# DeltaNet with a mixture of depths on one core: more filler products in TensorE's planned pauses, first k loads over two DMA queues, other planning costs

## Chip, cores, metric

The kernel runs on one NeuronCore of a Trainium2 chip, in one launch. The metric is the device time of that launch in microseconds, the median of its runs. Before the change it is 312.81 us (three runs, 311.75 to 313.92).

## What is computed

Attention of the DeltaNet kind over 4 batches, 8 heads, 768 tokens and a head size of 48, all in fp32, then a feed-forward block that only the 128 best-scored tokens of each batch pass through.

```python
k_n = k / (np.linalg.norm(k, axis=-1, keepdims=True) + 1e-06)
for t in range(S):                                    # S = 768
    y[:, :, t] = einsum('bhd,bhde->bhe', q[:, :, t], state)
    v_old = einsum('bhde,bhd->bhe', state, k_n[:, :, t])
    state += beta[:, :, t] * einsum('bhd,bhe->bhde', k_n[:, :, t], v[:, :, t] - v_old)
x = y.transpose(0, 2, 1, 3).reshape(B, S, H * D)      # 4 x 768 x 384
for b in range(B):
    scores = x[b] @ w_gate
    top = the 128 tokens with the highest scores
    h = maximum(x[b, top] @ w1, 0)                    # 384 x 1024
    out[b, top] = x[b, top] + sigmoid(scores[top]) * (h @ w2)
```

## The kernel before

**Tiling.** The tokens are cut into chunks of 64, 12 per sequence. Two batches are worked on together, so there are 24 steps, each one chunk of 16 heads and batch pairs. Within a chunk the token-by-token recurrence becomes a triangular system. Four steps form one elimination, of which there are six: each inverts 32x32 triangular blocks on VectorE by 30 column steps of two instructions (`step`, L760 and L764), on the copy in PSUM that ScalarE makes (`fill`, L737). There is only one such PSUM tile, `pa`.

**A step's course.** `load` (L539, L542) brings k, q and v, two DMAs each, one for each half of the partitions. `turn` transposes k and q on TensorE (L560), ACT copies them out (L564). `products_g` (L578) and `products_p` (L588) make k k^T and k q^T; ACT copies them to `g` (L598) and `p` (L602), GpSimd masks `p` (L609). `eliminate` scales the block on GpSimd (L724; on VectorE for elimination 0), opens with L737, runs its steps, and ends with L783 and the transposes L789 and L795. `join` completes each 64x64 inverse with 32x32 products (L907, L919), which ACT copies (L913, L925). `recur` is the recurrence: v scaled by the norms on GpSimd (L951), L976 and L961 (v minus what the state holds), L993 (times the inverse), ACT's copy L998 to `wbd`, L1006 (new state), L1022 and L1033 (the output), ACT's copy L1039, the output DMA L1043. `depths` picks the tokens of a batch and runs the feed-forward block (L1276 and L1290), after an indirect gather (L1260); a scatter that adds (L1299) ends it.

**What sets the order.** All instructions are issued by a planner in the kernel itself, `Plan`, when the kernel is built. Each operation has an engine, a cost in us that is written by hand, dependences and the buffers that it takes and gives back. `rank` makes 90 trial orders with priorities that partly come from a seeded random source and keeps the one whose planned end is earliest; `order` makes it. Costs thus do not only describe: a changed cost gives another order on every engine. Each engine then takes its instructions strictly in the planned order, whatever the real times are.

**Fillers.** `Plan.fill` goes over TensorE's planned order. `near` is the activity of the last 3.4 us of plan, each operation weighted with a hand-written `rate`. Where it is under a threshold, a filler is put in: two products of `warm` with itself (L1389), 128x128 in bf16, whose result nobody reads. They have no dependences and run as soon as TensorE comes to them.

The two helpers that carry a load are these:

```python
n["l" + nm] = moved(sp, 1.3, 1.5, load(i, nm), prio=u - 30 + (nm == "q") * 34,
                    take=[(nm, i)], lat=2.5)
n["mp"] = pool(1.1, mask_p(i), [n["w", 0], n["w", 1], N["masks"]], 10 * i - 10)
r["vh"] = pool(1.05, vh, [n["lv"], N["e", e]["nn"]], u - 8)
```

`moved` plans an issue on SP (1.3 us for the two DMAs), then the transfer (1.5 us) and a latency (2.5 us). A second path of `eliminate`, with 16-row quarters, is written out but its list of eliminations, `PARTED`, is empty.

Of the kernel before, what the change touches and what calls it, by code (L numbers as in the profile page):

```python
# [16 lines left out]
P = 128  # L17
# [15 lines left out]
class Plan:  # L33
# [61 lines left out]
    def fill(self):  # L95
# [5 lines left out]
        for op in ops + [None]:  # L101
            end = op.start if op else last
            here = 0
            while t + 0.12 < end or here < 2:
                if any(a < t < b for a, b in used):
                    if t + 0.12 >= end:
                        break
                    t += 0.1
                    continue
                near = sum((min(y, t) - max(x, t - 3.4)) * r for x, y, r in work[-60:]  # L110
                           if y > t - 3.4)
                if near < 2.8 and (t > 3.4 or t + 0.12 < end):
                    fill = Op()
                    fill.eng, fill.start, fill.end, fill.give, fill.seq = "PE", t, t, [], -1
                    fills.append(fill)
                    work.append((t - 0.11, t, 3.2))
                    here += 1
                elif t + 0.12 >= end:
                    break
                if t + 0.12 < end:  # L120
                    t += 0.12
# [147 lines left out]
def kernel(  # L269
# [64 lines left out]
    QC = HC // 2  # L334
    QD = QC * HC + QC
    NW = 3
    SUMS = ()
    PARTED = ()
# [22 lines left out]
    ring("a", 2, [HC * HC + QC * 2])  # L361
# [70 lines left out]
    zq = sbuf("zq", [NB // 2, QC, 2])  # L432
    identb = sbuf("identb", [P], BF16)
    low_i = sbuf("low_i", [GP, QC], BF16)
# [41 lines left out]

    def quarters():
        nc.gpsimd.tensor_copy(identb, ident)
        for x in range(2):
            nc.gpsimd.tensor_tensor(out=low_i[:, x], in0=ident[:, x * C + QC:x * C + HC],  # L480
                                    in1=ident[:, x * C + HC + QC:(x + 1) * C], op=ALU.add)
        nc.gpsimd.tensor_tensor(out=low_i[:, 0], in0=low_i[:, 0], in1=low_i[:, 1], op=ALU.add)
        nc.gpsimd.tensor_copy(low_i[:, 1:], low_i[:, :1].to_broadcast([P, GP - 1, QC]))
# [48 lines left out]
    def load(i, nm):  # L532
        g, c = divmod(i, NCH)

        def emit():
            t = got(nm, i)
            for x in range(2):
                if nm == "v":
                    nc.sync.dma_start(out=t[half[x]], in_=v[g * GB + x, :, c * C:(c + 1) * C]  # L539
                                      .rearrange("h s d -> s h d"))  # L540
                else:
                    nc.sync.dma_start(  # L542
# [4 lines left out]
    N = {}  # L547

# [86 lines left out]
    def prep(i):  # L635
# [3 lines left out]
        for nm in "kq":  # L639
            n["l" + nm] = moved(sp, 1.3, 1.5, load(i, nm), prio=u - 30 + (nm == "q") * 34,  # L640
                                take=[(nm, i)], lat=2.5)
# [15 lines left out]
        n["mp"] = pool(1.1, mask_p(i), [n["w", 0], n["w", 1], N["masks"]], 10 * i - 10)  # L657
# [8 lines left out]
    def eliminate(e):  # L666
# [4 lines left out]
        parted = e in PARTED  # L671
# [4 lines left out]
        def quarter(t):  # L676

            return (t[:, :2 * QD].rearrange("p (s x) -> p s x", x=QD)[:, :, :QC * HC]
                    .rearrange("p s (i c) -> p s i c", c=HC)[:, :, :, :QC])

        def turn_in():
            nc.vector.transpose(
                out=rows(got("a", e)[:, :HC * HC]).rearrange("p t (n x) -> p t n x", x=2),
                in_=got(*gk(e))[:, :, HC:].rearrange("p n t x -> p t n x"))

        def square():
            eng.tensor_scalar_max(nrm[:, 0], got("a", e)[:, :HC * HC:HC + 1], 1e-30)
# [17 lines left out]
        def clear():  # L705
            if parted:
                for x in range(2):
                    a = quarter(got("a", e))[:, x]
                    nc.gpsimd.affine_select(out=a, in_=a, pattern=[[1, QC], [-1, QC]], base=0,
                                            channel_multiplier=0, compare_op=ALU.is_gt, fill=0.0)  # L710
                return
            a = rows(got("a", e)[:, :HC * HC])
# [3 lines left out]
        def scale():  # L716
            if parted:
                a = quarter(got("a", e))
                eng.tensor_tensor(
                    out=a, in0=a, op=ALU.mult, in1=bh[e % 2].rearrange("p (s i) -> p s i", s=2)  # L720
                    [:, :, :, None].to_broadcast([P, 2, QC, QC]))
            else:
                a = rows(got("a", e)[:, :HC * HC])
                eng.tensor_tensor(out=a, in0=a, op=ALU.mult,  # L724
                                  in1=bh[e % 2][:, :, None].to_broadcast([P, HC, HC]))
            eng.memset(got("a", e)[:, :HC * HC:HC + 1], -1.0)

        def state():

            return (got("A", e)[:, :QC].rearrange("p i c -> p (i c)")  # L730
                    .rearrange("p (s i c) -> p s i c", s=2, c=QC))

        def fill():
            if parted:
                nc.scalar.copy(state(), quarter(got("a", e)))
                return
            nc.scalar.copy(got("A", e), rows(got("a", e)[:, :HC * HC]))  # L737

        def step_q(j):
            w = QC - 1 - j  # L740

            def emit():
                a, x = quarter(got("a", e)), state()
                t = tmp[:, :2 * w * j].rearrange("p (s i c) -> p s i c", s=2, c=j)
                nc.vector.tensor_tensor(
                    out=t, op=ALU.mult,
                    in0=a[:, :, j + 1:, j:j + 1].to_broadcast([P, 2, w, j]),
                    in1=x[:, :, j:j + 1, :j].to_broadcast([P, 2, w, j]))
                nc.vector.tensor_tensor(out=x[:, :, j + 1:, :j], in0=x[:, :, j + 1:, :j],
                                        in1=t, op=ALU.subtract)  # L750
            return emit, 0.42 + 1.9e-3 * 2 * w * j

        def step(j):
            w = HC - 1 - j

            def emit():
                a = rows(got("a", e)[:, :HC * HC])
# [10 lines left out]
        def final():  # L768

            if parted:  # L770
                a = got("a", e)
                for x in range(2):
                    i0 = x * QC * HC
                    nc.vector.tensor_tensor(
                        out=a[:, i0:i0 + QC * HC].rearrange("p (i y) -> p i y", y=2 * HC)
                        [:, :, x * HC:(x + 1) * HC].rearrange("p i (c x) -> p i x c", x=2),
                        in0=state()[:, x].rearrange("p (i x) c -> p i x c", x=2), op=ALU.mult,
                        in1=bh[e % 2][:, None, None, x * QC:(x + 1) * QC]
                        .to_broadcast([P, QC // 2, 2, QC]))
                    nc.vector.memset(a[:, i0:i0 + QC * HC].rearrange("p (i y) -> p i y", y=2 * HC)  # L780
                                     [:, :, HC - x * HC:2 * HC - x * HC], 0.0)
                return
            nc.vector.tensor_tensor(  # L783
                out=got("a", e)[:, :HC * HC].rearrange("p (i c x) -> p i x c", c=HC, x=2),
# [3 lines left out]
        def turn_out():  # L788
            nc.vector.transpose(  # L789
                out=got("tt", e)[:, :, HC:].rearrange("p n t x -> p t n x"),  # L790
                in_=got("a", e)[:, :HC * HC].rearrange("p (i c x) -> p i x c", c=HC, x=2))

        def turn_back():
# [3 lines left out]
                in_=got("a", e)[:, :HC * HC].rearrange("p (i c x) -> p c i x", c=HC, x=2))  # L797

        def keep():

            nc.gpsimd.tensor_copy(zq, got(*gk(e))[:, :, HC:HC + QC])
# [16 lines left out]
        last = on((1.9 if e == 0 else 2.2) * (0.55 if parted else 1), scale, [s["sc"], cl],  # L818
                  -650 if e else u)
        if parted:  # L820
            s["kp"] = pool(0.8, keep, [s["in"], N.get("jq")], -640)
        last = act(0.6 if parted else 1.0, fill, [last], -600, take=[("A", e)])
        for j in range(1, (QC if parted else HC) - 1):
            emit, dur = (step_q if parted else step)(j)
            last = dve(dur, emit, [last, N.get(("e", e - 1), {}).get("tb")], u)
        s["fi"] = last = dve(1.4 if parted else 1.25, final, [last], u, give=[("A", e)])
        s["to"] = last = dve(1.3, turn_out, [last], u, take=[("tt", e)])
        s["tb"] = last = dve(1.3, turn_back, [last, s.get("kp")], u, give=[("a", e)])
        for m in range(BC):
            if parted:  # L830
                join_q(e, m)
            s["mv", m] = pool(0.7, move(m), [N["clear"], N[e * BC + m].get("eq_j", s["to"])], -640)
        for m in range(BC):
            join(e, m)

    def join_q(e, m):

        i = e * BC + m
        u = 40 * e - 25 + m
        s, n = N["e", e], N[i]  # L840
        at = slice(m * GP // 2, (m + 1) * GP // 2)
        quad = [slice(x * HC, (x + 1) * HC) for x in range(4)]

        def view(w, c):
            return got("inv", i, w)[:, :GP * c].rearrange("p (n x t) -> p n x t", x=2, t=c)

        def right(t, a, b):
            return t[:, at, a:b].rearrange("p n t x -> p n x t")

        def z():  # L850

            tt, ps, l = got("tt", e)[:, at], view("zq", QC), zq[:, at]
            nc.tensor.matmul(got("inv", i, "zq")[:, :GP * QC], lhsT=identb,
                             rhs=low_i.rearrange("p n t -> p (n t)"), start=True, stop=False,
                             skip_group_check=True)
            for f in range(GP):
                for x in quad:
                    nc.tensor.matmul(ps[x.start:x.start + QC, f // 2, f % 2],
# [584 lines left out]
```

## Time and profile before

| | |
|---|---|
| median of 3 runs | 312.81 us |
| the profiled execution, and its span | 322.07 us, 320.4 us |
| PE busy, and its weight loads | 285.2 us (89%), 235.1 us (73%) |
| VectorE, ACT, POOL busy | 199.9, 171.4, 150.2 us |
| mean granted TensorE clock | 0.885 |
| DMA, mean over the span | 82 GB/s, 26.21 MB in 87,923 packets |
| filler products L1389 | 208, 23.4 us busy |
| the chain that ended last | PE 73%, ACT 7%, issue 5%, DMA 5%, SP's queue 5% |
| eliminations open (ACT L737) at | 21.59, 52.60, 87.31, 118.21, 152.73, 186.92 us |

Busy time of PE is not its peak: products are pipelined and their ends are modelled. The granted clock is the share of the full TensorE clock that the throttle let through. The chain is followed back from the last instruction, each time to what released it.

### The profile page before, as it was taken

What the parts mean: (1) busy time and instruction counts of PE and PEld (TensorE: products, weight loads), DVE (VectorE), ACT (ScalarE), POOL (GpSimd) and SP (SyncE); (2) the same over time, 40 slices, a digit from 0 to 9 for tenths busy, and PEclk for the clock granted to TensorE, in tenths of its full rate; (3) what the DMA queues carried; (4) which work ended last, traced back from release to release, by engine and by line L of the source; (5) the groups of instructions that cost most, each with busy time, mean ns of one, the idle gap of its engine ahead of it and who ended that gap; (6) DMA issues with size and microseconds to landing.
All of it is one profiled execution on the core that took longest, in us unless ns stands there. A gap on an engine that the chain in (4) does not pass through costs nothing.

```text
span 320.4 us, 15640 instructions
## 1 busy us (share of the span) xinstructions
PE 285.2 (89%) x6896; PEld 235.1 (73%) x6896; DVE 199.9 (62%) x630; ACT 171.4 (54%) x381; POOL 150.2 (47%) x232
## 2 busy tenths in 40 slices
PE   6977577999999988998999898999999989999990
PEld 5756466778778877887778787877887777777870
DVE  6549994999089949956792879964208668372000
ACT  3866233436775775577666774674367672222210
POOL 7192749833662593258523694329033742021201
PEclk9979685559999997899957997997599999999996
DMA  5775778225442443556433521354020012032022
GB/s 99 139 129 100 131 139 241 36 50 109 109 94 55 98 103 83 103 96 142 122 71 69 104 71 39 93 106 129 24 51 29 29 58 70 0 51 25 28 25 25
DMA packets 87923, 26.21 MB, mean 82 GB/s; under 512 B 82448, under 2 KB 87280, under 8 KB 87856
## 3 DMA queue, kind: packets, MB, share of 16 engines
q1 hardware_dynamic: 86256, 23.54, 34.2%
q0 software_dynamic: 1600, 1.68, 3.4%
q8 instruction: 54, 0.88, 1.1%
q14 instruction: 13, 0.11, 0.1%
HBM read 18.38 MB, written 5.51 MB: 75 GB/s over the span
## 4 chain that ended last, share of the span: by engine, by line
PE 73%; ACT 7%; issue 5%; DMA 5%; SPq 5%; POOL 2%; POOLq 1%; DVE 0%; ACTq 0%
PE invs L976 7%; PE psta L1006 7%; PE invs L1033 7%; PE invs L560 6%; PE invs L993 5%; PE invs L1276 5%; PE invs L919 5%; PE invs L1290 5%; PE invs L961 5%; PE invs L907 4%; PE invs L1022 4%; SPq L542 4%; PE invs L578 3%; ACT wbd L998 3%; PE invs L588 3%
## 5 line engine op out<-in xcount | busy, mean ns | idle before, releaser
L760 DVE TENSOR_TENSOR tmp<-a,pa 128x30 f32<-128x30 f32 (+9 forms) x180 | 58.5, 325 | 29.7 <-ACT pa L737 24.0
L764 DVE TENSOR_TENSOR pa<-pa,tmp 128x30 f32<-128x30 f32 (+9 forms) x180 | 60.8, 338 | 6.2
L1047 POOL TENSOR_TENSOR xw<-x,wg 128x384 f32<-128x384 f32 x23 | 23.2, 1007 | 44.9 <-ACT x L1039 34.5
L951 POOL TENSOR_TENSOR v<-v,nnT 128x384 f32<-128x384 f32 x24 | 19.9, 828 | 40.2 <-DMA v<-in_v_dram 26.7
L609 POOL TENSOR_TENSOR p<-p,later 128x512 f32<-128x512 f32 x24 | 30.3, 1271 | 14.1 <-ACT p L602 13.8
L998 ACT COPY wbd<-invs 64x384 f32<-64x384 f32 x48 | 22.7, 472 | 12.4 <-PE invs L993 11.6
L1006 PE MATMUL psta<-wbd,k 128*48 128x96 f32 x352 | 23.6, 283 | 5.1 <-ACT wbd L998 3.8
L1389 PE MATMUL psta<-warm 128*128 128x128 bf16 x208 | 23.4, 252 | 1.7 <-DVE r L467 1.7
L1033 PE MATMUL invs<-wbd,p 128*64 128x96 f32 x384 | 24.1, 271 | 1.0 <-issue 1.0
L1006 PEld LDWEIGHTS psta<-wbd,k 128*48 128x48 f32 x352 | 18.5, 143 | 8.8 <-ACT wbd L998 6.2
L976 PE MATMUL invs<-v,ident 128*128 128x192 f32 x88 | 24.7, 412 | 0.0
L1276 PEld LDWEIGHTS invs<-xeT,w_sb 128*128 128x128 f32 x192 | 23.0, 192 | 2.2 <-issue 0.3
L1276 PE MATMUL invs<-xeT,w_sb 128*128 128x128 f32 x192 | 24.1, 278 | 0.0
L1290 PE MATMUL invs<-w_sb,hT 128*128 128x384 f32 x64 | 23.5, 492 | 0.0
L925 ACT COPY tt<-invs 32x256 f32<-32x256 f32 x48 | 18.4, 382 | 6.3 <-PE invs L919 4.9
L560 PE MATMUL invs<-ident,q 128*128 128x128 f32 x96 | 17.2, 307 | 5.0 <-DMA q<-in_q_dram 4.9
L564 ACT COPY qT<-invs 128x512 f32<-128x512 f32 x24 | 14.0, 586 | 12.9 <-PE invs L560 11.3
L1033 PEld LDWEIGHTS invs<-wbd,p 128*64 128x64 f32 x384 | 18.8, 149 | 2.8 <-issue 1.3
L807 POOL COPY tt<-tt 32x256 f32<-32x256 f32 x48 | 18.8, 392 | 2.3
L919 PE MATMUL invs<-g 32*32 32x32 f32 x640 | 17.1, 208 | 2.8 <-ACT g L913 1.8
L1012 ACT COPY s<-psta 128x384 f32<-128x384 f32 x22 | 10.5, 478 | 16.8 <-PE psta L1006 14.5
L984 ACT COPY r<-invs 128x384 f32<-128x384 f32 x22 | 10.5, 478 | 16.4 <-PE invs L961 16.0
(126 smaller groups left out, 576.2 us busy)
## 6 DMA issues: line engine op xcount, KB each, us to landing
k<-in_k_dram SPq DMA_DIRECT2D x48, 96.0 KB
q<-in_q_dram SPq DMA_DIRECT2D x48, 96.0 KB
v<-in_v_dram SPq DMA_DIRECT2D x48, 96.0 KB
out_dram<-x SPq DMA_DIRECT2D x24, 192.0 KB
w_sb<-in_moe_w_dram SPq DMA_DIRECT2D x3, 512.0 KB
w_sb<-in_moe_w_dram SPq DMA_DIRECT2D x4, 384.0 KB
g<-g SPq DMA_DIRECT2D x16, 64.0 KB
bt<-in_beta_dram POOLq DMA_DIRECT2D x24, 4.0 KB, 3.1
```

Source lines behind the costliest of these rows:

```text
L560: nc.tensor.transpose(ps[:, r * P:(r + 1) * P], x[:, 2 * r:2 * r + 2].rearrange("p b d -> p (b d)"), ident)
L609: nc.gpsimd.tensor_tensor(out=t, in0=t, op=ALU.mult, in1=later[:, None, :].to_broadcast([P, GP, C]))
L760: nc.vector.tensor_tensor(out=t, op=ALU.mult, in0=a[:, j + 1:, j:j + 1].to_broadcast([P, w, j]), in1=x[:, j:j + 1, :j].to_broadcast([P, w, ...
L764: nc.vector.tensor_tensor(out=x[:, j + 1:, :j], in0=x[:, j + 1:, :j], in1=t, op=ALU.subtract)
L919: nc.tensor.matmul(ps[lo[bb], f // 2, f % 2], lhsT=g[lo[bb], f // 2, f % 2, HC:], rhs=g[lo[bb], f // 2, f % 2, :HC], start=True, stop=True)
L976: nc.tensor.matmul(pv()[:, rt], lhsT=ident, rhs=heads(got("v", i))[:, rt], start=True, stop=False, skip_group_check=True)
L998: nc.scalar.copy(wb[half[par], :, par].rearrange("p (b m) d -> p b m d", b=2), pw()[half[par]])
L1006: nc.tensor.matmul(psta[ds[a % 2], a // 2], lhsT=t[:, a, :D], rhs=wb[:, a].rearrange("p h d -> p (h d)"), start=(c == 0 and a < 2), stop=True,
L1033: nc.tensor.matmul(y(rt)[half[bb], k].rearrange("p b d -> p (b d)"), lhsT=t[:, a], rhs=wb[:, a].rearrange("p h d -> p (h d)"), start=(c == ...
L1276: nc.tensor.matmul(got("inv", b, "h", f // 2)[:, f % 2 * CAP:(f % 2 + 1) * CAP], lhsT=w1_sb[:, t, f * P:(f + 1) * P], rhs=got("xeT", b)[:, ...
L1290: nc.tensor.matmul(got("inv", b, "o")[:CAP, :DM], lhsT=got("hT", b)[:, f], rhs=w2_sb[:, f], start=(f == 0), stop=(f == KF - 1))
L1389: nc.tensor.matmul(pfull[:, GI * 2 * D:], lhsT=warm, rhs=warm, start=False, stop=True, skip_group_check=True)
```

## The change

In `Plan.fill` the threshold of activity under which a filler is put in becomes 4.4 where the planned pause goes on for more than 0.12 us, and stays 2.8 otherwise. A new helper, `fetch`, issues all loads. For the k of steps 0 to 3 it issues the first half on SP and the second on ACT's queue; other loads stay on SP. The planning costs change: issue of a load 1.48 for 1.3, transfer 1.3 for 1.5, latency 2.2 for 2.5, mask 1.25 for 1.1, v 0.85 for 1.05, GpSimd's copy L807 0.87 for 0.7. The second feed-forward product (`mm_2`) waits for all four loads of w2 instead of the one with its rows. The quarter path and its tiles go.

```diff
-                if near < 2.8 and (t > 3.4 or t + 0.12 < end):
+                if near < (4.4 if t + 0.12 < end else 2.8) and (t > 3.4 or t + 0.12 < end):
...
+    SHARED = [(nm, i) for nm, m in (("k", 4), ("q", 0), ("v", 0)) for i in range(m)]
+    SIZE = 1.3
...
-    ring("a", 2, [HC * HC + QC * 2])
+    ring("a", 2, [HC * HC])
...
-    def load(i, nm):
+    def load(i, nm, parts=range(2), eng=nc.sync):
...
-            for x in range(2):
+            for x in parts:
...
+    def fetch(i, nm, prio):
+
+        if (nm, i) not in SHARED:
+            return moved(sp, 1.48, SIZE, load(i, nm), [], prio, [(nm, i)], lat=2.2)
+        a = sp(0.75, load(i, nm, [0]), [chain.get(nm)], prio, [(nm, i)], lat=0.05)
+        b = act(0.75, load(i, nm, [1], nc.scalar), [a], prio, lat=0.3)
+        chain[nm] = a
+        return plan.add("DMA", SIZE, lambda: None, [b], 0.0, lat=2.2)
...
-            n["l" + nm] = moved(sp, 1.3, 1.5, load(i, nm), prio=u - 30 + (nm == "q") * 34,
-                                take=[(nm, i)], lat=2.5)
+            n["l" + nm] = fetch(i, nm, u - 30 + (nm == "q") * 34)
...
-        n["mp"] = pool(1.1, mask_p(i), [n["w", 0], n["w", 1], N["masks"]], 10 * i - 10)
+        n["mp"] = pool(1.25, mask_p(i), [n["w", 0], n["w", 1], N["masks"]], 10 * i - 10)
...
-            s["mv", m] = pool(0.7, move(m), [N["clear"], N[e * BC + m].get("eq_j", s["to"])], -640)
+            s["mv", m] = pool(0.87, move(m), [N["clear"], s["to"]], -640)
...
-        n["lv"] = moved(sp, 1.3, 1.5, load(i, "v"), prio=10 * i - 25, take=[("v", i)], lat=2.5)
-        r["vh"] = pool(1.05, vh, [n["lv"], N["e", e]["nn"]], u - 8)
+        n["lv"] = fetch(i, "v", 10 * i - 25)
+        r["vh"] = pool(0.85, vh, [n["lv"], N["e", e]["nn"]], u - 8)
...
-            last = pe(0.65, mm_2(f), [hs[f // 2], last, N["w2", f // 2 * 2]], u, rate=1.6,
+            last = pe(0.65, mm_2(f), [hs[f // 2], last] + [N["w2", t] for t in range(0, KF, 2)], u, rate=1.6,
```

Counted in the two built programs: TensorE issues 482 filler products instead of 208; ACT issues four DMAs where it issued none; every other kind of product has the same count.

## Prediction

> **What bounds the kernel now.** I read the 40-slice table of the page first, because the edit concerns TensorE's clock, then stretches of time cut where that clock changes, then the chain that ended last, then the timeline of the start.
>
> ```profile
> span 320.4 us, 15640 instructions
> ...
> PE   6977577999999988998999898999999989999990
> ...
> PEclk9979685559999997899957997997599999999996
> ```
>
> PE is busy in most slices, and PE holds 73% of the chain. The clock row has holes. Cut at their edges, the stretches are these (columns: from:to, length, then busy time and count of PE, its weight loads, DVE, ACT and POOL, then the granted clock, DMA share, GB/s):
>
> ```profile
> 18.00:22.00 4.00, 4.00 (x74) 3.12 (x74) 0.24 (x2) 2.10 (x4) 4.00 (x8) 0.57 0.81 137
> 35.00:42.00 7.00, 6.06 (x84) 4.88 (x84) 6.55 (x16) 2.35 (x5) 5.56 (x11) 0.52 0.72 130
> 48.50:73.00 24.50, 21.59 (x432) 18.14 (x432) 18.73 (x50) 9.04 (x22) 17.28 (x43) 0.51 0.44 108
> 123.50:131.00 7.50, 7.50 (x147) 6.06 (x140) 6.89 (x18) 3.76 (x9) 1.44 (x2) 0.54 0.27 61
> 161.50:172.00 10.50, 10.04 (x224) 8.48 (x223) 8.56 (x22) 5.93 (x15) 2.82 (x3) 0.51 0.33 70
> 195.50:199.50 4.00, 4.00 (x48) 3.50 (x52) 3.69 (x10) 1.47 (x4) 1.67 (x3) 0.57 0.05 13
> 219.50:233.50 14.00, 14.00 (x258) 12.06 (x258) 6.05 (x25) 5.57 (x14) 4.23 (x10) 0.51 0.29 82
> ```
>
> Seven stretches, 71.5 us, run at about half clock. In the last five PE is busy nearly all the time, so a slow product there is a longer kernel. The price of one cold microsecond comes from the chain: sixteen L1006 products took 1.52 us cold and 0.87 warm, four L976 1.58 and 0.85, sixteen L1033 1.48 and 0.81. Cold work takes about 1.8 times as long, so a cold microsecond loses about 0.44.
>
> Before 54 us something else binds: one elimination must end before the recurrence can start, and the second cannot start until its inputs are scaled.
>
> ```profile
> 13.14 4.72 DMA k<-in_k_dram
> ...
> 18.00 0.96 PE invs L560 x4
> ...
> 21.69 0.92 ACT pa L737
> ...
> 42.27 4.15 DMA v<-in_v_dram
> 46.55 0.83 POOL v L951
> 47.38 2.47 POOL p L609 x2
> ...
> 50.45 1.92 POOL a L724
> 52.60 1.02 ACT pa L737
> 53.62 0.32 ACT g L913
> 53.99 1.07 PE invs L919 x32
> ```
>
> The reader is to see two things in this chain (start, length, what). The last k loads leave SP up to 18.5 us, and their late transposes hold up ACT's copy L737, which opens elimination 0: it starts at 21.59 although VectorE had its input ready at 18.34 (L726). And elimination 0 ends at 47.06 (L783, 45.83 plus 1.23), but L737 of elimination 1 runs only at 52.60: POOL waited for v of step 3, multiplied it, masked two p, and only then scaled. The first joins' ACT copies L913 stand behind that L737.
>
> **What the skill says.** (1) "TensorE: Matmul & The Clock Gate", section on the HAM clock gate: the array runs at half clock until about 3.4 us of activity releases it, and falls back after an idle window. The trace agrees on the quantum: integrated over half-microsecond stretches, the seven cold stretches hold 3.4, 6.8, 23.9, 6.8, 10.2, 3.4 and 13.7 us, multiples of 3.4. It does not fit plain idleness: from 48.5 to 73 PE was busy 21.59 of 24.5 us and stayed cold. The stretches from 48.5 on begin among or just after the 32x32 products L907 and L919, which use little of the array. (2) The same page's table at its end asks for no PE gap over about 3 us; the cold stretch at 35 follows one of 4.39 us before an L560, so this agrees. (3) "DMA: Bandwidth & Descriptors", "Issuing engines are not separate DMA queues": a second issuing engine saves only issue time, the 16 DMA engines are shared. Here they are 58% to 78% busy in the first three 8 us stretches, so there is something to save, but not everything.
>
> **The change part by part.** Time is counted against the profiled execution (322.07 us, of which 320.4 is the span), which is 9.26 above the median of 312.81. The page does not tell where those 9.26 went; the likeliest place is cold windows, and I charge them there: less cold time is left to win in a median run.
>
> *First k loads.* The second halves of k0 to k3 move from SP to ACT's queue. SP needs 0.68 us from issue to issue, so everything behind goes out 4 x 0.68 = 2.7 us earlier, k8 at 10.4 instead of 13.1 at its end. ACT issues only after its table load and one activation, which end at 2.30. ACT's issue cost is not in the trace; taken as SP's 0.65, its four end at about 5.0, before the kT0 copy at 5.80. Low bound 0; at double, 5.2 us, they end at 7.5 and delay that copy and all queued behind it on ACT, the kT and g copies, by 1.7. k0's own second half leaves 0.7 later than now (2.30 instead of 1.64), k3's 0.7 earlier. In the new ACT order L737 stands behind kT8, no longer behind kT9. VectorE's chain should be ready at about 17.1 (its transpose at 13.14 comes about 1.2 earlier, ACT being free of waits for k2 and k3), k8 lands at about 15 if the DMA engines keep up. Elimination 0 then opens at about 18.2: -3.4 us, between 0 and -5.
>
> *Replanned order of the second elimination.* The new costs (load 1.48, mask 1.25, v 0.85, move 0.87) give another order. On POOL, v3 and the masks p3 and p4 no longer stand between the norms and the scale: p1 to p5 and v1 come earlier and only v2 remains. v2 moves on SP from behind 48 DMAs to behind 50, with 2.7 us less of issue before it. What leaves POOL's path is 46.55 to 49.80, 3.3 us, and the 1.73 us wait for v3. What is late next: v2's landing, or ACT's root L690, which still stands behind qT6. Then L737 follows the end of elimination 0 by about 2 us and not 5.5: -3.6, between +2 and -5.5. Together the recurrence starts about 7 us earlier.
>
> *Fillers.* The threshold in a planned pause rises from 2.8 to 4.4. TensorE issues 482 filler products instead of 208. Of the 274 added, 94 lie before the first L1006 (228 instead of 134), where PE waits; 92 stand in one block ahead of the first L907. The trace prices them: 34 in a row took 2.06 us with the last one's 0.22, so 1.84 / 33 = 0.056 us each. The block is 5.2 us; it fits if TensorE's preparation ends 5 us before elimination 0. Now 34 run from 44.65 to 46.7, and the cold stretch starts after the 1.78 us wait that follows. The other 180 (254 instead of 74) cost 180 x 0.056 = 10.1 us if none is hidden, and 0 if each falls into a real wait. PE's idle time from 73 to 264, between cold stretches included, is about 12 us, and short waits for ACT lie under the products' modelled ends. I take +4.
>
> What they buy: the cold time on PE's path is 19 us (54 to 73) and 7.5 + 10.5 + 4 + 14 = 36, 55 us x 0.44 = 24 us. With 9.26 charged as above, some 15 remain in a median run. Fillers go only where the planner has a pause, so runs of 32x32 products without one stay as light as they are. I take a little over half: -8, between 0 and -15.
>
> *The rest.* L1290 now waits for all four w2 loads; the last one issues at 219.5 and the first L1290 runs at 269.6, so nothing, and that cover is 50 us deep. The removed quarter path is never called (its list of eliminations is empty): nothing; its tiles go, nobody waited for them. The order of steps after 55 us also changes, with equal amounts of work: +2, between -4 and +8, no view of the profile decides it. The end, from the last L993 at 244.4 to the end at 320.4, holds the same products: nothing.
>
> Sum: -7 + 4 - 8 + 2 = -9 against the median, 303.8; against the profiled execution the clock term may be -17, 304.
>
> **The rivals.** *Gains eaten* (0.15): the start gains 4, the clock 3, the fillers cost 6 and order 1: 312.8. For it: the cold stretch at 48.5 went on under a busy PE. *Fillers on the path* (0.15): the one that ends slower. TensorE takes instructions in order, so a filler whose planned pause is not there delays the product behind it, and through it ACT's copy. If 80% of the 180 count (+8), they run cold part of the time (+3, since four cold ones took 0.60 us), the new order costs 4, the clock gains 3 and the start 3, the result is 322; it decides from where fillers and order cost more than 11 us. Against it: PE waits at joins in every elimination. *The edit does not reach the clock* (part of the first): the 92 run off early, PE idles until the joins, and stays cold to about 66. *All cold gone* (0.10): clock -15, start -9, fillers +3, order 0: 292.
>
> **How the numbers follow.** The likeliest case (0.60) is 303.8, its own range 297 to 310. Range 294 to 317: it leaves out part of the best case and of the worst. Runs of this kernel lie within 0.4% of their median, so about 1% is what a measurement can tell from none. Faster by over 1% means under 309.7: most of the likeliest, all of the best: 0.69. Within 1%: 0.16. Slower: 0.15.
>
> **What would show it.** L737's first two starts: 18 and 46 (now 21.59 and 52.60). Half-clock time: under 45 us, above all less between 48 and 73. L993 products, 32 in 0.67 us there and not 1.08. Fillers with idle time still ahead of L907 mean a free block; no idle and late joins mean that they cost. If L737 of elimination 1 is still over 50, or cold time stays near 70, I am wrong.

## The result, and the profile after

The changed kernel takes 324.43 us in the median of four runs (322.51 to 325.32), the kernel before 313.37 (311.75 to 316.32). The ratio is 1.033 with a 95% interval of 1.024 to 1.043: slower. That ratio takes only the executions near each kernel's fastest, and one and the same program spreads over some 6% here, with TensorE's clock low in different stretches each time; with all executions of the study taken together the mean spans are 319.1 us (10 executions) and 313.2 (46), 1.9% apart. The profiled execution after took 324.93 us. This is its page, with the slices of PE and clock, the chain's shares, and the group of the fillers (busy time, mean ns of one, idle time before them):

```profile
span 323.2 us, 16191 instructions
...
PE   7979778999979998989989999999999999999990
...
PEclk9999796589989997989955999699999999999998
...
PE 78%; issue 5%; ACT 5%; DMA 4%; DVE 4%; POOL 2%; POOLq 1%; SPq 0%; DVEq 0%
PE psta L1266 7%; PE invs L557 7%; PE invs L910 6%; PE invs L853 6%; PE psta L883 6%; PE invs L870 6%; PE invs L796 5%; PE invs L1153 5%; PE invs L1167 5%; PE invs L784 4%; PE invs L899 4%; PE invs L838 4%; PE invs L585 4%; PE invs L575 4%; PE invs L1004 2%
...
L1266 PE MATMUL psta<-warm 128*128 128x128 bf16 x482 | 45.6, 243 | 1.7 <-DVE r L463 1.7
```

The same list of the chain before, in which the filler was L1389:

```profile
PE invs L976 7%; PE psta L1006 7%; PE invs L1033 7%; PE invs L560 6%; PE invs L993 5%; PE invs L1276 5%; PE invs L919 5%; PE invs L1290 5%; PE invs L961 5%; PE invs L907 4%; PE invs L1022 4%; SPq L542 4%; PE invs L578 3%; ACT wbd L998 3%; PE invs L588 3%
```

The clock is better: 0.916 on the mean, not 0.885. But the first item in the list of what the kernel's end hangs on is L1266, the filler, with 7%. Before, the filler is not among the fifteen named. Adding the pieces of the chain one by one from 58 us on, fillers hold 5.7 us before and 19.5 after. A filler has nothing that waits for its result; it is on the chain only because the product behind it on TensorE could already have run.

The cold stretches after (columns as in the prediction):

```profile
36.50:40.50 4.00, 3.91 (x79) 3.46 (x79) 3.72 (x10) 1.21 (x3) 2.75 (x4) 0.57 0.63 113
50.50:68.00 17.50, 17.36 (x379) 14.64 (x373) 16.09 (x45) 6.82 (x19) 7.80 (x30) 0.51 0.43 123
94.50:98.50 4.00, 4.00 (x71) 3.21 (x67) 3.69 (x10) 2.15 (x5) 1.27 (x1) 0.57 0.01 4
125.50:129.50 4.00, 4.00 (x108) 3.54 (x104) 3.66 (x10) 2.33 (x7) 0.80 (x1) 0.57 0.29 65
142.50:146.50 4.00, 4.00 (x34) 3.06 (x30) 0.00 (x0) 2.06 (x5) 2.57 (x3) 0.57 0.34 63
163.00:177.00 14.00, 12.96 (x246) 10.85 (x246) 11.66 (x30) 5.17 (x14) 1.83 (x2) 0.51 0.18 42
200.50:208.00 7.50, 7.50 (x134) 6.28 (x132) 6.92 (x18) 3.69 (x10) 4.87 (x5) 0.54 0.08 26
```

They are 55 us long together instead of 71.5. The largest, at 50.5, begins among the first joins, as the one at 48.5 did before. The timeline of TensorE ahead of it suggests why:

```profile
40.99 5.30 PE L1266 MATMUL psta<-warm 128*128 128x128 bf16 x92
49.74 2.27 PE L784 MATMUL invs<-tt,g 32*32 32x32 f32 x96 [3.45 <-DVE tt L732]
```

The planner spread 92 products over its pause. TensorE does not know the plan's times: it ran them off in 5.3 us and then stood idle for 3.45 us until VectorE's transpose; 0.8 us later the clock was at half (e8_block, below, tests whether the wait is the cause). In this pause, fillers meant as cover came too early; elsewhere, where the pause did not exist, they came in the way. This is the middle of that largest slow stretch, from the chain in order of time:

```profile
63.96 1.03 PE invs L838 x32
64.99 1.18 PE psta L1266 x10
66.18 1.48 PE invs L910 x16
```

Ten cold fillers took 1.18 us between two groups of real work that followed each other without a wait.

### The profile page after: what moved, and what is told of

It reads as the page before. It is cut to its first block, busy times and chain, and to the rows that moved or that the text cites. A ratio compares the mean times of both kernels' runs of the same rounds, so it can differ in the third digit from the quotient of the medians.

```text
span 323.2 us, 16191 instructions
## 1 busy us (share of the span) xinstructions
PE 294.5 (91%) x7170; PEld 246.3 (76%) x7170; DVE 198.9 (62%) x630; ACT 171.0 (53%) x381; POOL 149.3 (46%) x232
## 4 chain that ended last, share of the span: by engine, by line
PE 78%; issue 5%; ACT 5%; DMA 4%; DVE 4%; POOL 2%; POOLq 1%; SPq 0%; DVEq 0%
PE psta L1266 7%; PE invs L557 7%; PE invs L910 6%; PE invs L853 6%; PE psta L883 6%; PE invs L870 6%; PE invs L796 5%; PE invs L1153 5%; PE invs L1167 5%; PE invs L784 4%; PE invs L899 4%; PE invs L838 4%; PE invs L585 4%; PE invs L575 4%; PE invs L1004 2%
## 5 line engine op out<-in xcount | busy, mean ns | idle before, releaser
L1266 PE MATMUL psta<-warm 128*128 128x128 bf16 x482 | 45.6, 243 | 1.7 <-DVE r L463 1.7
L1266 PEld LDWEIGHTS <-warm 128*128 128x128 bf16 x482 | 33.7, 109 | 6.4 <-issue 1.6
L1153 PE MATMUL invs<-xeT,w_sb 128*128 128x128 f32 x192 | 25.8, 278 | 0.0
L1167 PE MATMUL invs<-w_sb,hT 128*128 128x384 f32 x64 | 25.3, 495 | 0.0
L853 PE MATMUL invs<-v,ident 128*128 128x192 f32 x88 | 23.0, 390 | 0.0
L883 PE MATMUL psta<-wbd,k 128*48 128x96 f32 x352 | 21.1, 268 | 0.9 <-ACT wbd L875 0.6
L585 PE MATMUL invs<-qT,kT 48*64 48x64 f32 x768 | 17.9, 232 | 2.7 <-issue 2.2
L883 PEld LDWEIGHTS psta<-wbd,k 128*48 128x48 f32 x352 | 16.4, 134 | 4.6 <-ACT wbd L875 3.2
L599 ACT COPY p<-invs 128x512 f32<-128x512 f32 x24 | 14.1, 587 | 10.4 <-PE invs L585 10.0
L1160 ACT ACTIVATE hT<-invs 128x256 f32<-128x256 f32 x16 | 6.1, 384 | 24.4 <-PE invs L1153 24.4
```

The costliest lines, as they stand in the source:

```text
L585: nc.tensor.matmul(small(i, "w", rt)[half[par], r // 2, r % 2], lhsT=t[ds[rt], r, half[par]], rhs=s[ds[rt], r, half[par]], start=True, sto ...
L853: nc.tensor.matmul(pv()[:, rt], lhsT=ident, rhs=heads(got("v", i))[:, rt], start=True, stop=False, skip_group_check=True)
L883: nc.tensor.matmul(psta[ds[a % 2], a // 2], lhsT=t[:, a, :D], rhs=wb[:, a].rearrange("p h d -> p (h d)"), start=(c == 0 and a < 2), stop=True,
L1153: nc.tensor.matmul(got("inv", b, "h", f // 2)[:, f % 2 * CAP:(f % 2 + 1) * CAP], lhsT=w1_sb[:, t, f * P:(f + 1) * P], rhs=got("xeT", b)[:, ...
L1167: nc.tensor.matmul(got("inv", b, "o")[:CAP, :DM], lhsT=got("hT", b)[:, f], rhs=w2_sb[:, f], start=(f == 0), stop=(f == KF - 1))
L1266: nc.tensor.matmul(pfull[:, GI * 2 * D:], lhsT=warm, rhs=warm, start=False, stop=True, skip_group_check=True)
```

## The experiments

**How they are compared.** Cold time is (1 - granted clock) x 2 x span, so that a microsecond at half clock counts as one. Within each kernel, span rises with it: 0.36 us per cold us (standard error 0.02, from all 128 executions of 15 kernels). So each kernel is given by its mean span, its mean cold time, and the span that the slope gives at 50 us of cold time. This takes a cold us that fillers remove to be worth as much as one that differs by chance, which no run shows by itself. The expectations were written as the study went on, with 0.35 and somewhat different values for the kernels known by then.

| run | order | filler products | executions | mean span | cold | span at 50 cold |
|---|---|---|---|---|---|---|
| before, with e0_before | old | 208 | 46 | 313.2 | 54.9 | 311.5 |
| e1_fill | old | 490 | 4 | 312.7 | 30.2 | 319.8 |
| e5_early | old | 304 | 6 | 314.5 | 47.1 | 315.5 |
| e7_late | old | 394 | 6 | 313.3 | 34.8 | 318.7 |
| e13_old_one | old | 348 | 6 | 315.5 | 49.8 | 315.6 |
| e15_old_join | old | 400 | 6 | 312.8 | 37.1 | 317.4 |
| e3_queues | old | 208 | 4 | 317.8 | 61.1 | 313.8 |
| after, with e12_after | new | 482 | 10 | 319.1 | 48.4 | 319.6 |
| e2_after_oldfill | new | 212 | 4 | 318.2 | 69.2 | 311.3 |
| e6_after_early | new | 308 | 6 | 316.6 | 62.8 | 312.0 |
| e8_block | new | 364 | 6 | 320.2 | 56.8 | 317.7 |
| e9_one | new | 351 | 6 | 314.8 | 58.6 | 311.8 |
| e10_three | new | 613 | 6 | 318.4 | 31.4 | 325.0 |
| e11_sync | new | 482 | 6 | 321.4 | 55.7 | 319.4 |
| e14_new_join | new | 404 | 6 | 319.1 | 50.3 | 319.0 |

With six executions a mean span is uncertain by about 2 us; at equal cold time by about 1. Each group of runs had the kernel before beside it on the same chip. At 50 us of cold time it lies at 311.4 in the group of e0 to e3, 313.0 with e5 to e8, 310.5 with e9 to e12 and 311.0 with e13 to e15, so kernels of one group compare best.

**Which part costs.** First the kernel before again:

> The kernel before, unchanged, to have a second profile of it: all theories expect a ratio of 1.00 (within 0.5%). The first profiled execution was 9 us above the median of its kernel with 68 us of cold clock. If cold clock explains the 9 us, an execution near 313 us has about 20 us less of it, some 48 us.

Its four runs went from 305.77 to 319.94 us, with a median of 318.34 beside 313.84 in its group, 1.4% off where 0.5% was expected. So the spread of one kernel is itself the size of the effect, and the cold time goes with it (the fastest had 30 us of it, the profiled one 64). The spread that I had read as "within 0.4%" came from three runs.

```diff
# e1_fill: the kernel before
-                if near < 2.8 and (t > 3.4 or t + 0.12 < end):
+                if near < (4.4 if t + 0.12 < end else 2.8) and (t > 3.4 or t + 0.12 < end):
```

> The kernel before with the new threshold of the fillers alone (4.4 in a planned pause); the order of everything else is the same on every engine. Theory F (the added fillers delay TensorE): 320 to 325 us, ratio 1.02 to 1.04. Theory O (the new order costs, the fillers are free): 311 to 315 us, ratio within 1% of 1. Theory Q (the two queues at the start cost): the same as O.

```diff
# e2_after_oldfill: the changed kernel
-                if near < (4.4 if t + 0.12 < end else 2.8) and (t > 3.4 or t + 0.12 < end):
+                if near < 2.8 and (t > 3.4 or t + 0.12 < end):
```

> The changed kernel with the old threshold of 2.8: two queues, new costs and so the new order, but the old fillers. Theory F: 310 to 315 us. Theory O: 320 to 326 us, ratio 1.02 to 1.04. Theory Q: 320 to 326 us too.

```diff
# e3_queues: the kernel before, in load
-                    nc.sync.dma_start(
+                    eng = nc.scalar if nm == "k" and i < 4 and x == 1 else nc.sync
+                    eng.dma_start(
```

> The kernel before with the second halves of k0 to k3 issued on ACT's queue and nothing else; the planned order of all other instructions stays. Theories F and O: 310 to 314 us, elimination 0 opens up to 3 us earlier than in the kernel before. Theory Q: 318 us or more, elimination 0 opens later.

The medians are 315.11, 320.03 and 320.58 us, beside 313.84. They contradict F in the first two, fit O in these within 0.2 us, and fit the times of Q in all three. But elimination 0 did not open later in e3_queues, as Q says: at 19.50, where the two profiles of the kernel before have 21.59 and 19.56. Four executions can't tell the 2.4 us of e3_queues at equal cold time from chance, and e11_sync below speaks against Q.

Two things add up in the raw times. At equal cold time the threshold alone costs 8.3 us in the old order (319.8 against 311.5) and 8.3 in the new one (319.6 against 311.3), as F says, and the new order costs nothing. This can be seen without the slope: the five executions of the kernel before with the least cold time (29 to 37 us) had spans of 301.8 to 306.9, the four of e1_fill, with 22 to 37 us of it, 307.3 to 316.8. The other thing is the cold time itself. In the old order the fillers take away 25 us of it, in the new one 21, and so about pay for themselves: the mean span goes from 313.2 to 312.7 and from 318.2 to 319.1. The new order has 14 us more cold time to begin with, and in raw time it is this that makes the changed kernel slower: 318.2 us with the old fillers against 313.2, from four executions.

**Which fillers cost.** The thresholds of e5_early, e7_late and e6_after_early are limited by the plan's time:

```diff
# e5_early: the kernel before. e6_after_early: the changed kernel, with t < 50
+                if near < (4.4 if t + 0.12 < end and t < 46 else 2.8) and (t > 3.4 or t + 0.12 < end):
# e7_late: the kernel before
+                if near < (4.4 if t + 0.12 < end and t >= 46 else 2.8) and (t > 3.4 or t + 0.12 < end):
```

> The kernel before, with the threshold of 4.4 only in the first 46 us of the plan: 96 of the added filler products, nearly all ahead of the first L1006. Each run is compared at its cold time, (1 - granted clock) x 2 x span, with 0.35 us of span for each cold us, the slope of the first 28 executions. Theory F (fillers after the first L1006 lie on TensorE's path, those before it are free): at 50 us of cold time a span of 311 to 313 us, as the kernel before (311.5). Theory G (fillers cost wherever they are): 315 to 317.

> The kernel before, with the threshold of 4.4 only after the first 46 us of the plan: 186 added products. Theory F: at 50 us of cold time a span of 319 to 321 us, as with all of them (319.6). Theory G: 315 to 317. Theory W (they lie in real waits and cost nothing): 311 to 313. Cold time itself: 30 to 45 us, since the stretches after 73 us go.

> The changed kernel with its threshold of 4.4 only in the first 50 us of the plan. Theory F: at 50 us of cold time 311 to 313 us (the changed kernel: 321.1); cold time about 55 to 69 us, so spans of 312 to 318. Theory G: 314 to 316 at 50 us of cold time.

In the new order the 96 early products are free (312.0 against 311.3) and the 174 behind them cost 7.6 us (319.6 against 312.0), as F says. In the old order e5_early, at 315.5, is where G has it, and e7_late, at 318.7, just under F's range; neither theory holds for both. Against the kernel before in their own group, 313.0, the early 96 cost 2.5 us and the late 186 cost 5.7, together as much as all of them in e1_fill. So the late ones cost most in both orders, and that the early ones are free isn't shown for the old one.

**Is the idle window the cause of the first cold stretch?** In e8_block, e6_after_early gets 28 fillers (56 products) more, right ahead of the first product L784. This is the pause in e6_after_early:

```profile
39.33 5.30 PE L1266 MATMUL psta<-warm 128*128 128x128 bf16 x92
49.60 2.77 PE L784 MATMUL invs<-tt,g 32*32 32x32 f32 x96 [4.97 <-DVE tt L732]
```

```diff
+            for _ in range(op.extra):
+                filler()
...
+        if i == 0:
+            n["z"].extra = 28
```

> As the run before, with 56 more filler products (3.1 us) right ahead of the first L784, where TensorE stood idle from 46.3 to 49.7 us in the changed kernel before its clock fell at 50.5. If that idle window starts the cold stretch (17 us of it), the stretch goes or is 7 us or less, and the span is 4 to 6 us shorter than in the run before. If the 32x32 products themselves bring it, it stays at 14 to 20 us, and the spans are equal within 2 us.

The timeline of TensorE in e8_block (the line numbers are those of this kernel) shows the pause covered, with 0.41 us left:

```profile
40.06 8.43 PE L1271 MATMUL psta<-warm 128*128 128x128 bf16 x148
48.90 1.72 PE L787 MATMUL invs<-tt,g 32*32 32x32 f32 x96 [0.41 <-DVE tt L735]
```

And its clock, in the stretches where it was low up to 148 us:

```profile
56.00:63.50 7.50, 6.40 (x128) 5.29 (x123) 6.92 (x18) 2.69 (x7) 2.60 (x14) 0.54 0.24 44
90.00:118.00 28.00, 25.58 (x519) 22.16 (x520) 14.96 (x39) 12.49 (x29) 7.31 (x9) 0.51 0.26 54
131.00:148.50 17.50, 16.60 (x320) 13.84 (x314) 16.16 (x42) 8.21 (x19) 3.55 (x4) 0.51 0.34 67
```

The joins ran warm: 96 products L787 in 1.72 us, not 2.77. Half clock added up over half-microsecond stretches, e6_after_early has 17 us of cold behind them and e8_block 6.8, as expected. That is one profile, but the other sixteen of this study all have 10 to 24 us there. The time did not shrink: in this execution 27 us of cold appeared at 90, and over six executions the mean span was 3.6 us longer, not 4 to 6 shorter. One covered window does not keep the clock up further on. At equal cold time the 56 products go with 5.7 us (317.7 against 312.0), more than the 3.1 that they take, though they lie in a pause. No view explains this, so a comparison at equal cold time can be off by some us.

**The price of one filler.** Same places, other size, in the changed kernel; e12_after is the changed kernel itself on that chip.

```diff
             if op.seq < 0:
-                filler()
+                filler(1 if op.start >= 50 else 2)
...
-    def filler():
-        for _ in range(2):
+    def filler(n):
+        for _ in range(n):
```

e10_three has 3 in the place of 1.

> The changed kernel again, to have more of its runs beside those below on one chip: mean span 320 to 324 us, mean cold time 50 to 60 us, ratio to the kernel before 1.015 to 1.035.

> The changed kernel with one product in each filler after the first 50 us of the plan and two before: 131 products fewer (351), at the same places. Theory F (they lie on TensorE's path, 0.056 us each): up to 7.3 us less at equal cold time, 4 to 7 by 0.35 us for each cold us; cold time goes up to 60 to 68 us, which takes 2 to 5 us back, so a span 0 to 5 us under the changed kernel's. Theory W (they lie in real waits): equal at equal cold time, so 2 to 5 us longer.

> The same with three products in each late filler: 131 more (613). Theory F: 4 to 7 us longer at equal cold time; cold time falls to 25 to 45 us, so a span between 4 us under and 3 us over the changed kernel's. Theory W: cold time falls as much and nothing is paid, 4 to 10 us shorter.

At equal cold time: 311.8 us with 351 products, 319.6 with 482, 325.0 with 613. Against e12_after alone, which ran beside the other two and lies at 318.7, the steps are 6.9 and 6.3 us for 131 products each, 0.053 and 0.048 us a product; one warm filler takes 0.056. They are on TensorE's path nearly whole. The chains agree: from 58 us on fillers hold 9.8, 19.5 and 26.4 us of them in the profiles of one, two and three. The cold times, 58.6, 48.4 and 31.4, move as F said, the first a little less than expected. e12_after itself had a mean span of 316.8 and 44.7 us of cold time, less than expected in both; the kernel before had 313.3 beside it. In raw span the three of this chip are 314.8, 316.8 and 318.4. This is the page of e10_three:

```profile
span 318.5 us, 16453 instructions
...
PEclk9998995699979999999959997999999999999996
...
L1266 PE MATMUL psta<-warm 128*128 128x128 bf16 x613 | 52.0, 235 | 2.3 <-DVE r L463 1.7
```

Its mean clock is 0.944, against 0.885 in the first profile of the kernel before, and its span is shorter than that one's by only 1.9 us.

**The two queues.** In e11_sync both halves go out on SP and all else keeps its planned order.

```diff
-        b = act(0.75, load(i, nm, [1], nc.scalar), [a], prio, lat=0.3)
+        b = act(0.75, load(i, nm, [1], nc.sync), [a], prio, lat=0.3)
```

> The changed kernel with both halves of k0 to k3 on SP, the planned order of all else kept. In the changed kernel the first transpose started at 5.97 us, 0.8 later than in the kernel before, and the first L672 at 14.97, 1.8 later. If ACT's queue is the cause, the first transpose starts at 5.1 to 5.4 again and L672 at 13.5 to 14.2, while L707 opens later, at 21 to 23 us, since k8 is issued 2.7 us later. If the 12 fillers behind the first transpose are, L672 stays at 14.7 or later. The end moves by under 2 us either way.

L672 starts at 14.17 us in e11_sync, where the expectation had it if ACT's queue is the cause. But it starts at 14.15 in e12_after too, with ACT's queue: the 14.97 was one profile's, and ACT's queue is not why L672 is later than before (13.14). L707 opens elimination 0 at 22.07; in the eight profiles of the new order with both queues it opens at 19.25 to 20.20. So the second queue brings 1.9 to 2.8 us there. Nothing is left of it when elimination 1 opens: 49.88, against 48.80 to 50.35 in those eight. At equal cold time the ends are level (319.4 and 319.6). The mean span is 4.6 us longer than that of e12_after, with 11 us more cold time, so the expected end within 2 us holds at equal cold time alone; Q, for which going back to SP should gain, is not met.

**The joins, and a better version?**

```diff
# e13_old_one: the kernel before, threshold 4.4, and
+                filler(1 if op.start >= 46 else 2)
# e14_new_join and e15_old_join: thresholds of e6_after_early and e5_early, and one filler
# behind each group L784, L796 (old: L907, L919)
+        n["z"].extra = n["j"].extra = 1
```

> The kernel before in its own order, with the threshold of 4.4 and one product in each filler after the first 46 us of the plan: 348 products, 50 more than before after the first L1006. Theory F: at 50 us of cold time 312 to 316 us; cold time 40 to 52 us, so spans 309 to 314, level with the kernel before or up to 4 us better.

> The changed kernel's order with the old threshold after 50 us of the plan (as in e6_after_early) and one filler of two products behind each of the 48 groups of 32x32 join products: 96 more products, 5.4 us. Theory J (the joins, light on the array, are what makes the clock fall in the new order): cold time falls from 63 to 40 us or less, the span is 0 to 4 us shorter than 316.6. Theory K (the clock falls from something else, such as the shift against its window): cold time stays over 55 us and the span is 3 to 6 us longer.

> The same in the kernel before's order (as e5_early, 96 more products behind its joins). Theory J: cold time falls from 47 to 35 us or less, span 0 to 4 us shorter than 314.5. Theory K: cold time stays within 7 us, span 3 to 6 us longer.

Against e6_after_early and e5_early the cold time falls by 12.5 us in the new order and by 10 in the old, less than J asked for in the first and nearly as much in the second; the spans are 2.5 us longer and 1.7 shorter, against an uncertainty of about 2 to 3. The two groups ran on different chips, and the kernel before had 5 us less cold time in the second. So the joins may have a share in the clock's fall, and what makes the new order colder stays open. e13_old_one was a miss in its span, 315.5 us and not 309 to 314, though its cold time and its 315.6 at equal cold time lay where expected. No version beat the kernel before by more than the uncertainty (e1_fill 312.7 and e15_old_join 312.8, against 313.2).

## Why the prediction was wrong

I had forecast 303.8 us, 9 less than before; the mean span came out 5.9 longer, so 15 us lie between. Three steps of the sum failed: the gain at the start (7 us forecast, nothing at the end), the fillers, of which I had hidden 60% in waits (they cost 4.3 us more), and the order, which I had given no cold time of its own (3.1). Neither of my two signs of being wrong came: elimination 1 opened at 49.56, not over 50, and cold time was 54 us in the profile after, not near 70.

*First k loads, -3.4.* The issue term held: forecast 2.7 us, 1.9 to 2.8 by e11_sync. But elimination 0 opened at 20.20 and 19.39 in the two profiles after, not 18.2, and 21.59 is not the start before: its second profile has 19.56. VectorE's transpose L672, forecast 1.2 us earlier than 13.14, came at 14.97 and 14.15; why isn't shown. ACT's issues didn't wait for its activation, as I had assumed: the first went out at 1.77, not 2.30, and the last ended at 6.04, ahead of the copy that I feared for (7.10).

*Second elimination, -3.6.* L707 ran at 49.56 and 49.05, not 46; before, at 52.60 and 50.56. And this gain didn't reach the recurrence. I had asked what is late between the norms and the scale, and named v2 or ACT's root. What was late came ahead of the norms: GpSimd itself, in its timeline:

```profile
39.46 2.29 POOL L423 DMA_DIRECT2D bt<-in_beta_dram  x4
41.77 0.84 POOL L828 TENSOR_TENSOR v<-v,nnT 128x384 f32<-128x384 f32 x1
42.56 1.28 POOL L606 TENSOR_TENSOR p<-p,later 128x512 f32<-128x512 f32 x1
43.93 0.32 POOL L677 TENSOR_SCALAR nrm<-a 128x32 f32<-128x32 f32 x1
```

L677 opens the norms; its input L672 was there at 40.88, and four beta DMAs, one v and one p stood ahead of it. The norms ended at 45.89. VectorE takes their reciprocal before the last steps of elimination 0, and so held elimination 0 for them, where before it did not wait:

```profile
45.92 0.35 DVE L687 RECIPROCAL bh<-nrm 128x32 f32<-128x32 f32 x1 [2.64 <-POOL nrm L683]
```

In the kernel before:

```profile
44.58 0.34 DVE L697 RECIPROCAL bh<-nrm 128x32 f32<-128x32 f32 x1
```

All eight profiles of the new order with both queues have this wait, 1.8 to 3.75 us; in e11_sync, which opens later, 0.48 of it is left. So an earlier opening of elimination 0 is lost in this wait. Elimination 0 takes 28.4 us in the mean of these eight from its opening to the end of its scaling (L783, now L726), and 25.8 in the seven profiles of the old order with the loads on SP. The recurrence starts (first L870, before L993) at 57.8 us in the mean of the one and at 58.3 of the other: 0.6 of the 7. The third elimination opens at 84.6 and 85.0.

*Fillers, +4 of at most 10.1.* The price of 0.056 us was right; that 60% would fall into waits was not. At equal cold time they cost 8.3 us. I had read "short waits under the modelled ends" as cover, and no view showed that these waits lie at the planned places.

*The clock, -8.* The fillers took away 21 us of cold time, and a cold microsecond costs 0.36: -7.5. The size was right by two errors that cancel: my price of 0.44 came from products on the chain alone, and the cold time that went is more than the 18 us which -8 stands for at that price.

*The order, +2.* Nothing at equal cold time, together with the start (-0.2). But the new order with the old fillers has 69.2 us of cold time (four executions) and the old one 54.9: 14.3 x 0.36 = +5.1. I had given the order no cold time; where it comes from stays open.

*Sum with the measured terms:* -0.2 + 8.3 - 7.5 + 5.1 = +5.7, beside 5.9. This splits the same means into parts and is no check of its own.

The rival "fillers on the path", with 322, came nearest, and had the fillers right (8). That its total is close is luck in part: its start gains 3 and its clock 3, where the runs show 0.6 or less and 7.5. The picture of "the edit does not reach the clock" came true at the first joins: the 92 ran off early, TensorE idled, and it stayed cold to 68.

## What to carry to other kernels

Work put in to hold a clock runs when its engine gets to it, not when the plan says: here it was early in a long pause (92 products in 5.3 us, then 3.45 idle) and in the way where the pause was missing. Price it in full, and set against it the cold time that it removes times the measured cost of a cold microsecond; here about 0.05 us a product against 0.36 a cold us came out even. When an order changes, ask what stands ahead of an operation that another engine waits for, and not only what stands behind it. And where the clock's fall differs from run to run, take many executions and compare at equal cold time, for three can agree by luck.

## What was unexpected of the hardware

One unchanged program had between 29 and 74 us of half clock and spans from about 302 to 320 us. Apart from the last microseconds of a run, the cold time comes in steps of 3.4 us: the stretches of the profile after hold 3.4, 17.1, 3.4, 3.4, 3.4, 13.7 and 6.8. TensorE can stay at half clock for many such steps while it is busy nearly all the time with small products: 17.36 of 17.5 us from 50.5, 12.96 of 14.0 from 163. In sixteen of the seventeen profiles a stretch of 10 us or more of it begins at 46.5 to 52.5 us, about where the first joins run; the other is e8_block.
